# Attention chunks in groups of one and two, with masks and value swaps placed by hand, in a fused retention and low-rank mixing kernel

## The chip, the cores and the metric

The kernel runs on one core of a Trainium2 chip. The time is device microseconds of one execution; the kernel before was timed three times. In the profile PE is TensorE's matmul row and PEld its weight loads, DVE is VectorE, ACT ScalarE, POOL GpSimd, SP the engine whose queue issues most transfers. A line number such as L513 is a line of the kernel before. All times below are microseconds unless marked ns.

## The reference

Shapes: q, k, v are 8 batches x 8 heads x 576 positions x 64; the model width is 512.

```
scores = scale * q @ k.T                       # per batch and head
gamma  = 1 - 2 ** (-5 - head)
ret    = scores * where(rel >= 0, gamma ** rel, 0)
x      = ret @ v                               # heads side by side: 576 x 512 per batch

h   = (x.T @ U) @ V                            # U 576 x 32, V 32 x 576
u   = x + h.T
out = u + relu(u @ w_ch1) @ w_ch2              # 512 -> 2048 -> 512
```

Inputs and output are float32; the kernel computes in bf16 and accumulates in float32.

## The kernel before, in words

**Tiling.** Two batches form a pair, `pr` = 0 to 3, and a pair's 1152 rows are cut into 9 chunks of 128 tokens, `i` = 0 to 8. Chunk 4 (`J`) holds the last 64 rows of the first batch and the first 64 of the second. The decay factors are folded into scalings of q's side (`qscale`, on the result) and of v (`vscale`), so attention is linear: within each half chunk of 64 rows a masked product of scores and values, and across half chunks a running state, a 64 x 64 matrix per head.

**One chunk's attention.** `load` (L230) brings q, k, v by the SP queue; `prep` casts them (q on ScalarE, k on VectorE or, from the seventh chunk of pair 1 on, on GpSimd), scales v on GpSimd, and `xbar` (L263) transposes q and k by a transfer that also stands in the SP queue. Then on TensorE, all in 64 x 64 tiles, four of which share the array: `SC` (L279, scores, 16 matmuls), `ST` (L290, the state's increments, 8 or 16), `QS` (L361, q times the state, 8 or 16), `RV` (L344, masked scores times values, 16). On VectorE: `states` (L323, L325, adds an increment to the running state `s_f`, two half chunks per chunk, each from the one before), `XS` (L372, scales the result into `x`), `mask` (L303, four instructions of 64 x 256 from PSUM to `ret`), `swap_v` (L315, two copies that bring each half of v to the other 64 partitions, where RV reads them as `vs`). On ScalarE: `cast_states` (L334, the states in bf16, `s_sb`).

**A section.** `section(new, last)` joins the scores and increments of chunk n+1 with the products of chunk n: SC, ST, states, QS, RV, XS, mask, swap_v, in that order. So the masks and swaps of a chunk stand at the end of one section, and the next section's RV reads them. A full section has 64 small matmuls. PSUM: `psc` two banks (scores left, increments right), `po` two banks, `pss` one, and three banks `ps_big`, tag `big`.

**The large products.** For each batch `y1_items` makes 16 items, each the relu of 128 of the 2048 hidden columns for all the batch's chunks (4 chunks for an even batch, `par` 0, one PSUM bank; 5 for an odd one, two banks); ScalarE empties them (L518). `y2_items` makes for each chunk 4 items of 4 matmuls 128x512 into one bank, then one VectorE add (L536, `o_sb`) and a store from GpSimd's queue (L539). Both take their banks from `big`. An item carries its nominal time: 864 ns for 4 matmuls of 512 columns, 1080 ns for a Y1 item with five chunks.

**Mixing.** `MA` (L427) sums x.T U over a batch's chunks and ScalarE copies it (`a_sb`, L433); `MH` (L454) multiplies by V for groups of up to four chunks, and VectorE adds x (L460) into `u`; `MT` transposes u by a transfer on the SP queue (`uT`). An even batch has one group, an odd one two, (4,5,6) and (7,8).

**The order.** The engines' queues follow the program's order (`manual_schedule`). Startup and a first stretch make pair 0's attention and the first Y1. Then for b = 1 to 7 the large products of batch b are the `main` list, and `merge` drops the attention and mixing of batch b+1 between its items: each filler has a place, a share of the list's nominal time, and is issued before the first item at which that share is done. `places` does the same for loads and preps. Batch 1's list is 10 leftover Y1 items, then the Y2 items of batches 0 and 1 (41.9 us nominal); an even batch has 27.6, an odd one 34.6, and the Y1 half comes first. Fillers of before: sections and state casts alternate at equal steps over the first part of each list, MA, the last cast and MH follow. A tile taken from a pool takes the buffer that was released first in program order.

Of the kernel before, what the change touches and what calls it, by code (L numbers as in the profile page):

```python
# [9 lines left out]
FP32 = mybir.dt.float32  # L10
BF16 = mybir.dt.bfloat16
# [25 lines left out]
def kernel(  # L37
# [56 lines left out]
    s_f = consts.tile([P, 2, NHP * D], FP32, name="s_f")  # L94
# [21 lines left out]
    def early_consts():  # L116
# [39 lines left out]
        nc.vector.memset(sblk, 0.0)  # L156
# [115 lines left out]
    def SC(pr, i):  # L272
        c = ch[pr, i]
        qkT = c["qkT"]
        psc = ps_sc.tile([P, 2, 2 * SW], FP32, tag="psc", name="psc")
        for hp in range(NHP):
            for t in HALVES:
                for hl, r in enumerate(HALVES):
                    nc.tensor.matmul(  # L279
                        psc[t, hl, hp * D:(hp + 1) * D], qkT[r, NHP + hp, t],  # L280
                        qkT[r, hp, t], start=True, stop=True,
                    )
        c["psc"] = psc

    def ST(pr, i, steps):
        c = ch[pr, i]
        for hp in range(NHP):
            for hl, r in enumerate(HALVES):
                for t in steps:
                    nc.tensor.matmul(  # L290
                        c["psc"][r, t, SW + hp * D:SW + (hp + 1) * D],
                        c["qk"][HALVES[t], 1, hp * P + hl * HALF:hp * P + (hl + 1) * HALF],
                        c["v"][HALVES[t], 2 * hp + hl, :], start=True, stop=True,
                    )

    def mask(pr, i):
        c = ch[pr, i]
        tile_ = ret_pool.tile([P, H, P], BF16, tag="ret", name="ret")
        ret = tile_.rearrange("p h n -> p (h n)")[:, 0:2 * SW].rearrange(
            "p (t hp i) -> p t hp i", t=2, i=D)  # L300
        for hl, o in enumerate(HALVES):
            for n, t in enumerate(HALVES):
                nc.vector.tensor_tensor(  # L303
                    out=ret[o, n],
                    in0=c["psc"][t, hl, 0:SW].rearrange("p (hp i) -> p hp i", i=D),
                    in1=tri[t, None, t].to_broadcast([HALF, NHP, HALF]), op=ALU.mult,
                )
        c["ret"] = ret
# [8 lines left out]
    def states(pr, i, steps):  # L317
        c = ch[pr, i]
        f = s_f
        for t in steps:  # L320
            inc = c["psc"][:, t, SW:2 * SW]
            if (i, t) in ((0, 0), (J, 1)):
                nc.vector.tensor_copy(out=f[:, t, :], in_=inc)  # L323
            else:
                nc.vector.tensor_tensor(  # L325
                    out=f[:, t, :], in0=inc,
                    in1=f[:, 1 - t, :], op=ALU.add)
        c["s0"] = st.get("s_sb")

    def cast_states(pr, i, steps):  # L330
        w = slice(steps[0], steps[-1] + 1)
        st["s_sb"] = ch[pr, i]["s1"] = s_pool.tile(
            [P, 2, SW], BF16, tag="s_sb", name="s_sb")
        nc.scalar.activation(  # L334
            out=ch[pr, i]["s1"][:, w, :], in_=s_f[:, w, :], func=AF.Copy)

    def RV(pr, i):
        c = ch[pr, i]
        inter = q_steps(i)
        for hp in range(NHP):  # L340
            for t in range(2):
                for hl, r in enumerate(HALVES):
                    vt = c["v"][r, 2 * hp + hl, :] if t == hl else c["vs"][r, hp, :]
                    nc.tensor.matmul(  # L344
                        c["po"][HALVES[t], hl, hp * D:(hp + 1) * D],
                        c["ret"][r, t, hp, :], vt,
                        start=(hp == 0 and t not in inter), stop=True,
                        skip_group_check=True,
                    )

    def q_steps(i):
        return (1,) if i == 0 else (0,) if i == J else (0, 1)

    def QS(pr, i):
        c = ch[pr, i]
        c["po"] = ps_o.tile([P, 2, dm], FP32, tag="po", name="po")
        for hp in range(NHP):
            for t in q_steps(i):
                for hl, r in enumerate(HALVES):
                    s_sb = c["s1"][:, 0, :] if t == 1 else c["s0"][:, 1, :]  # L360
                    nc.tensor.matmul(  # L361
                        c["po"][HALVES[t], hl, hp * D:(hp + 1) * D],
                        c["qkT"][r, hp, HALVES[t]], s_sb[r, hp * D:(hp + 1) * D],
                        start=(hp == 0), stop=True, skip_group_check=True,
                    )

    def XS(pr, i):
        c = ch[pr, i]
        if ("x", pr) not in st:
            st["x", pr] = x_pool.tile([P, NI, dm], BF16, tag="x", name="xt")  # L370
# [756 lines left out]
```

## Time and profile before

| what | us |
|---|---|
| three runs, median (lowest to highest) | 319.9 (319.54 to 320.24) |
| span of the profiled execution | 318.7 |
| TensorE busy, L547 (Y2) and L513 (Y1) in it | 311.4, of which 126.3 and 132.2 |
| VectorE busy; L303 (masks), L315 (swaps) | 169.1; 45.3, 14.3 |
| ScalarE busy; L518 (Y1 drains), L334 (state casts) | 136.7; 89.1, 15.5 |
| lists of batch 1 / 2 / 3 / 4 / 5 / 6 / 7 begin near | 59 / 106 / 138 / 178 / 210 / 249 / 281 |

A row of the profile's groups reads: line, engine, operation, output <- inputs, partitions x elements and type, count, busy time, mean ns of one, then the idle time before them and what ended it. Matmuls overlap in TensorE's pipeline, so their mean ns is not what each one costs: that is read from the distance of their starts. In the chain of waits each piece has a start, a length and what ran; "issue" is time in which an engine waited for nothing that the profile shows.

### The profile page before, as it was taken

To read this page: it belongs to the slowest core of one execution; us is meant where nothing else is said; L and a number is where in the kernel's file an instruction comes from. 1 tells how busy PE (TensorE), PEld (TensorE's weight loads), DVE (VectorE), ACT (ScalarE), POOL (GpSimd) and SP (SyncE) were. 2 spreads that over 40 slices of the span, in tenths; PEclk is the share of its full clock that TensorE was granted. 3 is DMA by queue.
4 is the path that set the end of the run, shared out by engine and by line. 5 is a ranking of instruction groups with operands and counts; after the bars stand their busy time and mean duration, and the time that the engine had idled before them with its cause. 6 is when DMAs were issued, how large, how long until landed. Compare 5 with 4: busy or idle time off the path is not lost.

```text
span 318.7 us, 9166 instructions
## 1 busy us (share of the span) xinstructions
PE 311.4 (98%) x3929; PEld 167.7 (53%) x3929; DVE 169.1 (53%) x354; ACT 136.7 (43%) x293; POOL 90.3 (28%) x138
## 2 busy tenths in 40 slices
PE   8999899999999999999999999999999999999996
PEld 3564554554444444466644444466644444467544
DVE  5571466447995467545684468545674563500012
ACT  2757557772120465038720375048720463057400
POOL 5762933512232423132241423141241300110000
DMA  7999999999999979699994999598994710620022
GB/s 202 258 204 267 232 198 203 191 203 187 237 212 216 260 156 175 137 242 183 176 184 106 262 177 175 142 248 172 163 202 109 189 37 1 135 81 0 2 84 81
DMA packets 151321, 53.30 MB, mean 167 GB/s; under 512 B 131985, under 2 KB 148753, under 8 KB 151281
## 3 DMA queue, kind: packets, MB, share of 16 engines
q1 hardware_dynamic: 144512, 40.40, 70.2%
q0 software_dynamic: 6768, 12.32, 16.2%
q8 instruction: 30, 0.49, 0.7%
q14 instruction: 11, 0.08, 0.1%
HBM read 36.85 MB, written 9.44 MB: 145 GB/s over the span
## 4 chain that ended last, share of the span: by engine, by line
PE 84%; DMA 7%; ACT 3%; DVE 2%; issue 1%; SPq 1%; POOL 1%; ACTq 0%
PE ps_y L513 37%; PE ps_y L547 35%; DMA stage_t<-in_q_dram 5%; DMA qkT<-qk 2%; PE psc L279 2%; PE ph L454 1%; PE po L344 1%; PE ps_y L558 1%; PE po L361 1%; SPq L595 1%; PE psc L290 1%; PE pa L427 1%; ACT qkT L639 1%; PE psc L656 1%; PE pst L628 1%
## 5 line engine op out<-in xcount | busy, mean ns | idle before, releaser
L518 ACT ACTIVATE y<-ps_y 128x384 bf16<-128x384 f32 (+2 forms) x192 | 89.1, 489 | 105.1 <-PE ps_y L513 104.6
L513 PE MATMUL ps_y<-uT,w_sb 128*128 128x512 bf16 (+3 forms) x768 | 132.2, 326 | 0.7 <-ACT uT L922 0.4
L547 PE MATMUL ps_y<-w_sb,y 128*128 128x512 bf16 x560 | 126.3, 379 | 0.0
L513 PEld LDWEIGHTS <-w_sb 128*128 128x128 bf16 x768 | 70.2, 98 | 51.0 <-issue 2.4
L547 PEld LDWEIGHTS <-y 128*128 128x128 bf16 x560 | 52.7, 98 | 61.3
L536 DVE TENSOR_TENSOR o_sb<-ps_y,u 128x512 f32<-128x512 f32 (+2 forms) x38 | 25.2, 663 | 66.3 <-PE ps_y L547 63.9
L303 DVE TENSOR_TENSOR ret<-psc,tri 64x256 bf16<-64x256 f32 x108 | 45.3, 419 | 1.1
L539 POOL DMA_DIRECT2D out_dram<-o_sb x31 | 17.3, 558 | 98.6 <-DVE o_sb L536 95.7
L255 POOL TENSOR_TENSOR vt<-stage_t,vscale 128x512 bf16<-128x512 f32 (+1 forms) x29 | 30.2, 1041 | 52.3 <-DMA stage_t<-in_v_dram 44.6
L325 DVE TENSOR_TENSOR s_f<-psc,s_f 128x256 f32<-128x256 f32 x42 | 17.8, 423 | 26.2 <-PE psc L290 12.9
L460 DVE TENSOR_TENSOR u<-ph,xt 128x1024 bf16<-128x1024 f32 (+3 forms) x24 | 21.8, 951 | 9.3 <-PE ph L454 9.3
L246 ACT ACTIVATE qk<-stage_t 128x512 bf16<-128x512 f32 x27 | 16.9, 626 | 21.1 <-DMA stage_t<-in_q_dram 15.2
L372 DVE TENSOR_TENSOR xt<-po,qscale 128x512 bf16<-128x512 f32 x27 | 18.4, 681 | 1.8 <-PE po L344 1.8
L244 POOL CAST qk<-stage_t 128x512 bf16<-128x512 f32 x20 | 12.3, 614 | 23.6 <-DMA stage_t<-in_k_dram 21.4
L334 ACT ACTIVATE s_sb<-s_f 128x512 bf16<-128x512 f32 (+1 forms) x27 | 15.5, 575 | 3.8 <-DVE s_f L325 3.8
L315 DVE COPY vs<-vt 64x256 bf16<-64x256 bf16 x54 | 14.3, 265 | 1.2
L664 DVE TENSOR_TENSOR ret<-psc,triU 128x1024 bf16<-128x1024 f32 x8 | 9.6, 1222 | 9.2 <-PE psc L656 9.2
L189 PE MATMUL pw<-ident 128*128 128x512 bf16 x34 | 11.5, 461 | 1.4 <-POOL ident masks.py:199 1.4
L613 POOL CAST qk<-stage_t 128x512 bf16<-128x512 f32 x16 | 9.6, 613 | 9.9 <-DMA stage_t<-in_q_dram 5.3
L323 DVE COPY s_f<-psc 128x256 f32<-128x256 f32 x6 | 2.5, 424 | 16.4 <-PE psc L290 11.3
L279 PEld LDWEIGHTS <-qkT 64*64 64x64 bf16 x432 | 5.6, 107 | 9.6 <-issue 8.5
L433 ACT ACTIVATE a_sb<-pa 128x128 bf16<-128x128 f32 x8 | 2.2, 277 | 18.0 <-PE pa L427 18.0
(112 smaller groups left out, 191.4 us busy)
## 6 DMA issues: line engine op xcount, KB each, us to landing
stage_t<-in_k_dram SPq DMA_DIRECT2D x32, 256.0 KB, 4.8
stage_t<-in_q_dram SPq DMA_DIRECT2D x32, 256.0 KB, 5.3
stage_t<-in_v_dram SPq DMA_DIRECT2D x32, 256.0 KB, 5.5
out_dram<-o_sb POOLq DMA_DIRECT2D x31, 256.0 KB, 4.3
w_sb<-in_moe_w_ch_dram POOLq DMA_DIRECT2D x4, 512.0 KB, 8.0
w_sb<-in_moe_w_ch_dram POOLq DMA_DIRECT2D x8, 256.0 KB, 5.8
stage_t<-in_k_dram SPq DMA_DIRECT2D x8, 128.0 KB, 5.1
stage_t<-in_q_dram SPq DMA_DIRECT2D x8, 128.0 KB, 5.5
```

Of the source, the lines that this page charges most:

```text
L246: nc.scalar.activation(out=t[rows, 0, :], in_=c["f", 0][rows].rearrange("p h d -> p (h d)"), func=AF.Copy)
L255: (eng or nc.gpsimd).tensor_tensor(out=c["v"][rows], in0=c["f", 2][rows], in1=vscale[rows, i, :, None].to_broadcast([n, H, D]), op=ALU.mult,)
L303: nc.vector.tensor_tensor(out=ret[o, n], in0=c["psc"][t, hl, 0:SW].rearrange("p (hp i) -> p hp i", i=D), in1=tri[t, None, t].to_broadcast( ...
L325: nc.vector.tensor_tensor(out=f[:, t, :], in0=inc, in1=f[:, 1 - t, :], op=ALU.add)
L334: nc.scalar.activation(out=ch[pr, i]["s1"][:, w, :], in_=s_f[:, w, :], func=AF.Copy)
L372: nc.vector.tensor_tensor(out=xt[:, i, :].rearrange("p (hp hl d) -> p hl hp d", hl=2, d=D), in0=c["po"][:, :, 0:NHP * D].rearrange("p hl ( ...
L460: nc.vector.tensor_tensor(out=st["u", par][:, i0 - base:i0 - base + n, w].rearrange("p s (c d) -> p c s d", c=2), in0=ph[k][:, :, 0:n, :], ...
L513: nc.tensor.matmul(ps[:, 0:n, :], w1_sb[:, cc, f * P:(f + 1) * P], st["uT", par][:, c0:c0 + n, cc, :], start=(cc == 0), stop=(cc == NCC - 1),)
L518: nc.scalar.activation(out=st["y1", par][:, f, c0 * P:(c0 + n) * P], in_=ps[:, 0:n, :].rearrange("p s t -> p (s t)"), func=AF.Relu)
L536: nc.vector.tensor_tensor(out=o_sb[:, 0:n], in0=ps[:, 0:n], in1=st["u", par][:, c, w], op=ALU.add)
L539: (nc.sync if last else nc.gpsimd).dma_start(out=out_flat[r0:r0 + P, w], in_=o_sb[:, 0:n])
L547: nc.tensor.matmul(ps, st["y1", par][:, f, c * P:(c + 1) * P], w2_sb[:, f, :], start=(f == 0), stop=(f == NF - 1),)
```

## The change

Sections take a group of one or two chunks. The 27 chunks of pairs 1 to 3 are cut into 16 groups, and each step of a group, S (section), C (state cast), M (masks), W (value swaps), has a place of its own in the lists. Inside a section the products of the last group now come ahead of the scores of the new one. A group of two puts its state increments into `pss` and a `big` bank, since its scores fill `psc`; a group of one keeps both in `psc`. Mixing in these lists uses `po` for MA, and `po`, `pss` and `big` for MH, with three VectorE adds instead of two. Loads and preps have new places. `x` becomes two tiles, one per batch; `s_f` and `s_sb` hold four half chunks; three small startup tables move into tiles that are free then.

```diff
-    iotaU = consts.tile([P, 2, P], FP32, name="iotaU")
+    iotaU = s_f[:, 0, :].rearrange("p (j i) -> p j i", j=2)
...
-    sblk = consts.tile([P, 4, NHP, P], BF16, name="sblk")
-    U_f = consts.tile([P, 5, R], FP32, name="U_f")
+    s_halves = [s_pool.tile([P, 4, NHP * D], BF16, tag="s_sb", name="s_sb") for _ in range(2)]
...
+    U_f = s_f[:, 1, 0:5 * R].rearrange("p (c r) -> p c r", r=R)
...
-        nc.vector.memset(sblk, 0.0)
+        for t in s_halves:
+            nc.vector.memset(t, 0.0)
...
+    def SC(new):
         psc = ps_sc.tile([P, 2, 2 * SW], FP32, tag="psc", name="psc")
+        for a, c in enumerate(new):
+            qkT = ch[c]["qkT"]
+            for hp in range(NHP):
+                for t in HALVES:
+                    for hl, r in enumerate(HALVES):
+                        nc.tensor.matmul(
+                            psc[t, hl, a * SW + hp * D:a * SW + (hp + 1) * D],
+                            qkT[r, NHP + hp, t], qkT[r, hp, t], start=True, stop=True,
+                        )
+        return psc
+
+    def ST(new, psc):
+        if len(new) == 1:
+            inc = [psc[:, t, SW:2 * SW] for t in range(2)]
+        else:
+            inc = [ps_s.tile([P, 2 * SW], FP32, tag="pss", name="inc0"),
+                   ps_big.tile([P, 2 * SW], FP32, tag="big", name="inc1")]
...
+    def mask(new, psc):
+        m = len(new) * NHP
...
                 nc.vector.tensor_tensor(
-                    out=ret[o, n],
-                    in0=c["psc"][t, hl, 0:SW].rearrange("p (hp i) -> p hp i", i=D),
-                    in1=tri[t, None, t].to_broadcast([HALF, NHP, HALF]), op=ALU.mult,
+                    out=ret[o, n, 0:m],
+                    in0=psc[t, hl, 0:m * D].rearrange("p (b i) -> p b i", i=D),
+                    in1=tri[t, None, t].to_broadcast([HALF, m, HALF]), op=ALU.mult,
                 )
...
-        c["vs"] = s_pool.tile([P, NHP, D], BF16, tag="vs", name="vs")
+        c["vs"] = s_pool.tile([P, NHP, D], BF16, tag="vs", bufs=4, name="vs")
...
+    def states(new, inc):
+        for a, (pr, i) in enumerate(new):
+            for t in k_steps(i):
+                s, src = 2 * a + t, inc[t][:, a * SW:(a + 1) * SW]
+                if (i, t) in ((0, 0), (J, 1)):
+                    nc.vector.tensor_copy(out=s_f[:, s, :], in_=src)
+                else:
+                    nc.vector.tensor_tensor(
+                        out=s_f[:, s, :], in0=src, in1=s_f[:, st["f_end"], :], op=ALU.add)
+                st["f_end"] = s
+
+    def cast_states(new):
+        s_sb = s_pool.tile([P, 4, SW], BF16, tag="s_sb", name="s_sb")
+        n = 2 * len(new)
+        nc.scalar.activation(out=s_sb[:, 0:n, :], in_=s_f[:, 0:n, :], func=AF.Copy)
...
+    def out_products(last):
+        po = ps_o.tile([P, 2, 2 * SW], FP32, tag="po", name="po")
...
+        for a, (pr, i) in enumerate(last):
+            c = ch[pr, i]
+            for hp in range(NHP):
+                for t in q_steps(i):
...
+        for a, (pr, i) in enumerate(last):
+            c = ch[pr, i]
+            for hp in range(NHP):
+                for t in range(2):
+                    for hl, r in enumerate(HALVES):
+                        vt = c["v"][r, 2 * hp + hl, :] if t == hl else c["vs"][r, hp, :]
...
     def section(new, last):
 
+        if last:
+            po = out_products(last)
         if new:
-            SC(*new)
-            ST(*new, k_steps(new[1]))
-            states(*new, k_steps(new[1]))
-        if last:
-            QS(*last)
-            RV(*last)
-            XS(*last)
+            psc = SC(new)
+            inc = ST(new, psc)
+        for a, c in enumerate(last):
+            XS(*c, po, a)
         if new:
-            mask(*new)
-            swap_v(*new)
...
+            states(new, inc)
+            return psc
...
+        def MH(grp, beside=False):
+            lo = ps_o.tile([P, 2, NHP, P], FP32, tag="po", name="ph0")
+            if beside:
+                ph = [(lo, (0, 1)),
+                      (ps_s.tile([P, 1, NHP, P], FP32, tag="pss", name="ph1"), (2,)),
+                      (ps_big.tile([P, 1, NHP, P], FP32, tag="big", name="ph2"), (3,))]
...
-        items.append(MA)
+        items.append(lambda: MA((ps_o, "po")))
         for grp in outs:
-            items.append(lambda grp=grp: (MH(grp), MT(grp)))
+            items.append(lambda grp=grp: (MH(grp, True), MT(grp)))
...
+        stream = [(pr, i) for pr in range(1, B // 2) for i in range(NI)]
+        groups, n = [], 0
+        for size in (1, 2, 2, 1, 2, 1) + 2 * (2, 2, 1, 2, 2):
+            groups.append(stream[n:n + size])
+            n += size
...
+        def step(kind):
+            n = done[kind]
+            done[kind] += 1
+            new = groups[n] if n < len(groups) else []
+            if kind == "S":
+                scores[n] = section(new, groups[n - 1] if n else [])
+            elif kind == "C":
+                cast_states(new)
+            elif kind == "M":
+                mask(new, scores[n])
+            else:
+                for c in new:
+                    swap_v(*c)
+
         places = {
-            1: ((0.11, 0.24, 0.41, 0.53, 0.95), (0.06, 0.20, 0.32, 0.47, 0.60, 0.73)),
-            2: ((0.05, 0.18, 0.30, 0.95), (0.09, 0.29, 0.40, 0.52)),
...
+            1: ((0.11, 0.24, 0.41, 0.53, 0.70, 0.85),
+                (0.06, 0.20, 0.32, 0.47, 0.60, 0.73, 0.90)),
+            2: ((0.02, 0.14, 0.30, 0.55, 0.75), (0.05, 0.22, 0.40, 0.58, 0.85)),
+            3: ((0.02, 0.18, 0.36, 0.65, 0.90), (0.08, 0.25, 0.45, 0.62)),
+            4: ((0.15, 0.36, 0.55, 0.80), (0.05, 0.20, 0.45, 0.65, 0.88)),
+            5: ((0.02, 0.18, 0.36), (0.08, 0.25, 0.45, 0.62)),
+        }
+        fills = {
+            1: ("S.22 C.24 M.24 W.25 S.42 C.44 M.45 W.49 S.58 C.60 M.61 W.66 "
+                "S.70 C.73 M.74 W.80 S.96 C.98 M1 W1", (0.74, 0.78)),
+            2: ("S.25 C.28 M.27 W.30 S.52 C.55 M.75 W.80 S.90 C.94 M1 W1", (0.58, 0.64, 0.70)),
+            3: ("S.25 C.28 M.27 W.30 S.52 C.54 M.71 W.75 S.90 C.94 M1 W1", (0.58, 0.65)),
+            4: ("S.52 C.55 M.75 W.80 S.90 C.94 M1 W1", (0.58, 0.64, 0.70)),
+            5: ("S.25 C.28 M.27 W.30 S.52 C.54 M.71 W.75 S.90 C.94 M1 W1", (0.58, 0.65)),
+            6: ("S.20", (0.35, 0.45, 0.50)),
         }
```

In `fills` the letters are the steps with their places (shares of the list), and the numbers behind them are the places of MA and of each MH. "1" puts a step behind the list's last item. S.70 below means the section at 0.70 of its list.

More of the change, by code (lines that the diff above doesn't have):

```diff
@@ L296, in mask, with x_of, k_steps, q_steps @@
-    def mask(pr, i):
-        c = ch[pr, i]
+    def x_of(pr, i, n=None):
+        half = int(i >= J)
+        if ("x", pr, half) not in st:
+            st["x", pr, half] = x_pool.tile(
+                [P, NI - J if half else J, dm], BF16, tag=f"x{half}", name="xt")
+        t, l = st["x", pr, half], i - J * half
+        return t[:, l, :] if n is None else t[:, l:l + n, :]
+    def k_steps(i):
+        return (1,) if i == J else (0,) if i == NI - 1 else (0, 1)
+    def q_steps(i):
+        return (1,) if i == 0 else (0,) if i == J else (0, 1)
@@ L315, in swap_v @@
             nc.vector.tensor_copy(out=c["vs"][o], in_=v[HALVES[1 - hl], hl])
[L317 to L370, printed above, removed]
-        xt = st["x", pr]
+    def states(new, inc):
+        for a, (pr, i) in enumerate(new):
+            for t in k_steps(i):
+                s, src = 2 * a + t, inc[t][:, a * SW:(a + 1) * SW]
[5 more added lines that the diff above has]
+                st["f_end"] = s
@@ L1096 @@
             merge(main, fill, aux)
+        assert done["S"] == len(groups) + 1
         assert gl == len(order) and gp == len(order)
```

138 lines of the change are left out of this document (66 added, 72 removed), and 4 rows, old and new, of the table places.

## The prediction

> **What bounds the kernel now.** I read four views in this order: the busy table with the chain that ended last, that chain in order of time, TensorE's timeline through one attention section, and VectorE's timeline. The page first:
>
> ```profile
> PE 311.4 (98%) x3929; PEld 167.7 (53%) x3929; DVE 169.1 (53%) x354; ACT 136.7 (43%) x293; POOL 90.3 (28%) x138
> PE 84%; DMA 7%; ACT 3%; DVE 2%; issue 1%; SPq 1%; POOL 1%; ACTq 0%
> L761 DVE TENSOR_TENSOR ret<-psc,tri 64x512 bf16<-64x512 f32 x2 | 1.4, 689 | 5.2 <-PE psc L752 5.2
> ```
>
> TensorE is the bound; every other engine has half its time free on average. (The third line, from the groups by shape, is a price used below.) The chain in order of time (start, length, what) gives TensorE's own rates, and the places where it waits:
>
> ```profile
> 84.11 7.26 DMA qkT<-qk
> ...
> 131.11 7.01 PE ps_y L547 x32
> ...
> 142.80 0.46 ACT y L518
> 143.26 0.26 issue
> 143.52 0.62 ACT s_sb L334
> 144.14 0.52 ACT qk L246
> 144.66 0.39 ACT y L518
> ...
> 168.97 8.74 PE ps_y L547 x40
> ```
>
> 8 more Y2 matmuls cost 8.74 - 7.01 = 1.73 us, so 0.216 each, and 0.10 is left over per stretch (7.01 - 32 x 0.216). At 142.8 the chain leaves TensorE: two Scalar Engine jobs (cast of states, cast of q) stand between Y1 drains, and the Y1 stretch is 0.34 us longer than its matmuls. TensorE's timeline through a section:
>
> ```profile
> 145.61 0.32 PE L279 MATMUL psc<-qkT 64*64 64x64 bf16 x16
> 145.76 0.30 PE L290 MATMUL psc<-vt,qk 64*64 64x64 bf16 x16
> 145.89 0.30 PE L361 MATMUL po<-s_sb,qkT 64*64 64x64 bf16 x16
> ...
> 146.26 0.34 PE L513 MATMUL ps_y<-uT,w_sb 128*128 128x384 bf16 x1
> ```
>
> 16 small matmuls start in 0.13 us (145.76 to 145.89), so 64 take 0.52. From the first (145.61) to the next Y1 matmul (146.26) is 0.65, and with the 0.10 that each stretch carries a section costs 0.75, of which 0.23 is a price per section and not per matmul. VectorE's timeline behind a section, and one bad case with GpSimd beside it:
>
> ```profile
> 73.32 0.89 DVE L325 TENSOR_TENSOR s_f<-psc,s_f 128x256 f32<-128x256 f32 x2 [1.85 <-PE po L361]
> 74.12 0.68 DVE L372 TENSOR_TENSOR xt<-po,qscale 128x512 bf16<-128x512 f32 x1
> 74.72 1.72 DVE L303 TENSOR_TENSOR ret<-psc,tri 64x256 bf16<-64x256 f32 x4
> 76.47 0.46 DVE L315 COPY vs<-vt 64x256 bf16<-64x256 bf16 x2
> 76.96 0.69 DVE L536 TENSOR_TENSOR o_sb<-ps_y,u 128x512 f32<-128x512 f32 x1
> 77.56 0.42 DVE L244 CAST qk<-stage_t 128x512 bf16<-128x512 f32 x1
> ...
> 160.13 1.25 DVE L315 COPY vs<-vt 64x256 bf16<-64x256 bf16 x2
> ```
>
> ```profile
> 160.25 1.04 POOL L255 TENSOR_TENSOR vt<-stage_t,vscale 128x512 bf16<-128x512 f32 x1 [1.61 <-DMA stage_t<-in_v_dram]
> ```
>
> Start to start: states 0.45 where one adds to the other, x scaling (XS) 0.60, four masks 1.75, two swaps 0.49, output add 0.60, k cast 0.34. A pair doubles states, XS and swaps; its four masks become 64x512, the shape of L761, 0.69 each: 2.8.
>
> **The change, part by part.**
>
> Sections. The old plan runs 28 (27 chunks plus a last one without a new chunk); the new one has 16 groups, so 17. Matmuls per chunk stay the same in number and shape. Saved: 11 x 0.23 = 2.53 us. Bursts grow to at most 128 small matmuls, which no row shows. If they keep the rate, 2.53 stands; if the second half of the ten pair bursts started at half rate, it would cost 10 x 0.25 = 2.5 and nothing would be left. I take the full rate, since the four groups of 16 above show none slower than the first.
>
> Old waits that go. The 0.34 at 142.8 and its twin at 214.4: casts of states now come once in a Y1 stretch, alone, not beside a q cast; a lone cast costs 0.03 there (stretches from 146.26 and 151.35). Three times the second mixing group has waited for VectorE to empty the two tiles of the first: 8 mixing matmuls took 0.22 at 51.56 but 0.36 at 130.67, so 0.14; with three smaller tiles, freed in turn, two of the three vanish (batches 3 and 5). The section at 91.42 waited 0.18 for the qkT transfer issued at 84.11, which is covered by the wait below. Together 0.68 + 0.28 + 0.18 = 1.14.
>
> New wait 1, the fourth section of batch 1's stretch (S.70). Take t = 0 at the start of the section before it (S.58, at a chunk's end). On VectorE: output add 0.20 to 0.80, two XS to 2.0, three states to 3.25, a k cast still on VectorE for this chunk to 3.6, four wide masks to 6.4, the next output add to 7.0, then the swaps: first chunk done 7.5, second 8.0. TensorE needs 30 groups of 4 (0.96) + 0.23 = 1.19, six Y2 items of 0.864, and 0.19 for the state products: it wants the first swapped values at 6.56 and would finish at 6.82; it finishes at 8.14. Loss 1.3. The transfer of 84.11 lands at 91.4, when by these sums TensorE is at that section (91.3) and waiting anyway. W.66 stands behind the masks and the output add on one queue; that is the price of queueing it late. Bounds: 0 if VectorE is 1.3 faster, 2.1 if one swap is held up as at 160.13 (1.02 instead of 0.22).
>
> New wait 2, S.90 of batches 2 and 4 (masks at .75, swaps at .80): the same count puts the second chunk's swaps 0.3 after TensorE wants them. 2 x 0.3 = 0.6, bounds 0 to 2.2 (a held swap of 0.8 each).
>
> New wait 3, the last mixing. The two groups stand one Y1 item apart (.45 and .50, 15 and 16 items done), 0.96 us. VectorE's three adds for the first (128x768, 0.95; 128x384, an estimate of 0.55 between 0.42 for 256 and 0.68 for 512 columns) free the tiles after 1.1, 1.57 and 2.04. The second group waits 0.6, and the next Y2 chunk, whose PSUM buffer is the one freed last, 0.15. Against the 0.14 before: +0.6.
>
> New wait 4: S.96 stands one item before batch 2's Y1. Its second state tile sits in a Y1/Y2 bank until 2.93 after its start, when TensorE wants it at 2.72: 0.2. The double state cast (128x1024; L334 gives 0.62 for half of it, so about 1.1) is hidden, because Y1 with 4 chunks tolerates a drain 0.8 late; in batches 3 and 5 two more Y2 items lie between. Uncovered it would cost 0.5 each time.
>
> Costed at nothing, with their cover: products before scores (state casts, masks and swaps are all one section old); mixing first stage in the other bank (XS is done at 2.2 where it starts at 2.8); load and prep times moved (each load still stands 6 us or more before its prep, and median landing is 4.8 to 5.5 us; at the closest, batch 2's first load, a landing of 6.0, as of the q load issued at 112.57, would hold Y1's drains by some 0.5, within what they tolerate). The SP queue keeps its order up to the seventh transpose, past which one load (three DMAs, 2 us) moves, with 5 us to spare. GpSimd's queue is not reordered against its loads. The startup edits touch only where small tables lie; two memsets for one.
>
> **Sum.** -2.53 - 1.14 + 1.3 + 0.6 + 0.6 + 0.2 = -1.0 us. On the profiled execution's 318.7 us span that is 317.7. The runs' median, 319.9, lies 1.2 above this span, so 318.9 for the runs. A difference under 0.2%, 0.64 us, can't be told from none.
>
> **The Trainium skill** (SBUF — State Buffer, section "Who interferes with whom") says that VectorE copies in their fast modes and GpSimd share one port pair as an exclusive lock, and the later one blocks for a whole instruction. The trace agrees at 160.13: the swap beside GpSimd's 1.04 us instruction took 1.02, not 0.22. By that rule, this rival follows.
>
> **Rivals.** *Swaps held up by GpSimd (slower).* Swaps now end just ahead of the section that reads them, at S.58, S.70 and twice S.90. Each one that meets a GpSimd instruction adds 0.8 there: three of them make +2.4, so 321.3. It decides from two on (-1.0 + 1.6 = +0.6). For: 5 of the 54 swaps on VectorE's timeline were held up so, by 0.08 to 0.80. Against: near S.70 and S.90 GpSimd's scaling is done or waits behind an output store. Chance 0.17.
>
> *Banks in strict turn (slower).* If the three Y1/Y2 buffers went round in order rather than by first freed, the third Y2 chunk of batches 2 and 4 would need the buffer of the chunk just ended, whose output add stands behind the mixing adds: 1.25 each, 321.4. For: mixing and state tiles now share these three. Against: nothing else in the old Y stretches took buffers out of turn, so no row decides. Chance 0.07.
>
> *VectorE keeps up (faster).* If masks overlap as XS and output adds do (0.60 apart), or the sections come later than I count, waits 1 and 2 go: 318.9 - 1.9 = 317.0. For: VectorE is 53% busy. Against: the masks stand 0.44 apart for 0.42 each, so they don't overlap. Chance 0.14.
>
> *Long bursts lose what the merging saves (it doesn't do what it says).* With 0.1 per pair burst, or batch 1 paced by its transfers whatever the order, 1.0 is lost: 319.9. For: the transfers' share in that stretch is above 1 (16 engines' mean) and the chain passes through qkT there. Chance 0.12.
>
> **Chances.** Forecast 0.50, own range 318.2 to 319.7. Faster by 0.64: three quarters of the forecast, all of the third rival and little else, 0.53. Same: the rest of the forecast and most of the fourth, 0.23. Slower: both slow rivals, 0.24. The range that leaves out 2 in 10: 316.9 to 321.4.
>
> **What would show it.** Right: 17 bursts; pair bursts of 0.9 to 1.15 us; a gap of about 1.3 inside the products of S.70 that ends with L315's successor; mixing's last second group 0.8 instead of 0.36; no wait at the Y1 starts of batches 3 and 5. Wrong: swaps over 0.5 us ahead of a section, a wait of TensorE on an output add at a chunk's start, or burst rates above 0.032 us per four. I would be wrong most likely at VectorE's queue, whose order I counted by hand.

## The result, and the profile after

The kernel after takes 322.88 us (median of 20 runs, 320.81 to 327.06), the kernel before 320.35 (20 runs). The ratio is 1.0074 with an interval of 1.0046 to 1.0101: 0.7% slower, where 318.9 was forecast. Medians are over all runs of a kernel, and ratios leave disturbed executions of either kernel out, so the two can differ a little.

The profiled execution took 325.31 us with a span of 323.3, one of the slower of its 20. The page of the kernel after:

```profile
PE 309.7 (96%) x3903; PEld 169.8 (53%) x3929; DVE 167.6 (52%) x320; ACT 137.8 (43%) x282; POOL 90.6 (28%) x138
...
PEclk9999999999998999999999999999999999999999
...
PE 80%; DMA 7%; SPq 5%; DVE 5%; issue 3%; ACT 0%; POOL 0%; DVEq 0%
```

TensorE is still busy for some 310 us, so the change did not add work: the span grew by waiting. A line has appeared that the page before did not have, TensorE's granted clock, with a dip in slice 13. (26 matmul records are missing from this trace; the weight loads, 3929 as before, are complete, and stretches below are measured by them.) TensorE's waits from 60 us to the end, in total, times and longest:

```profile
PE po L388 <- DVE vs L340: 2.5, 2, 1.8
PE ps_y L559 <- issue: 2.4, 14, 0.3
PE psc L297 <- DMA qkT<-qk: 0.6, 1, 0.6
PE ps_y L525 <- DVE s_f L349: 0.2, 1, 0.2
PE ph L465 <- DVE u L471: 0.2, 1, 0.2
```

The second line is the missing records. The first is the section at .70 of batch 1 (S.70): its products of masked scores and values, RV (L388), wait for the swaps (L340). The chain in order of time shows that place:

```profile
91.80 0.69 DVE o_sb L548
...
92.52 0.22 DVE vs L340
...
92.75 0.22 DVE vs L340
...
93.01 0.55 DVE vs L340
93.56 0.01 issue
93.57 1.57 DVE vs L340
95.14 0.04 issue
95.18 0.31 PE po L388 x15
```

TensorE reached the swapped values at 92.2 and had them all at 95.2. Four equal swaps take 0.22, 0.22, 0.55 and 1.57. GpSimd's timeline says why:

```profile
92.78 0.58 POOL L551 DMA_DIRECT2D out_dram<-o_sb  x1 [4.70 <-DVE o_sb L548]
93.37 0.66 POOL L247 CAST qk<-stage_t 128x512 bf16<-128x512 f32 x1
94.01 1.03 POOL L258 TENSOR_TENSOR vt<-stage_t,vscale 128x512 bf16<-128x512 f32 x1
```

The output add at 91.80 stands just ahead of the swaps on VectorE. When it ends, it releases GpSimd's store, and behind the store wait the k cast and v scaling of chunk (1,7), the first chunk of pair 1 whose k GpSimd casts: they run beside the last two swaps and hold them up. The two waits are 0.84 and 2.02, together 2.9. The two held swaps took 0.33 and 1.35 longer than the 0.22 of the others, so 1.7 of the 2.9 is GpSimd's hold; the remaining 1.2 is VectorE's queue, which came to the swaps late. Then comes a second loss. Stretches of the trace (start and end, length, TensorE busy and its instructions, granted clock, transfer share, GB/s):

```profile
92.00:95.00 3.00, 0.70 (x41) 1.00 1.25 141
95.00:96.00 1.00, 0.63 (x47) 0.77 0.94 245
96.00:97.00 1.00, 0.86 (x3) 0.50 1.26 280
97.00:98.00 1.00, 1.00 (x4) 0.50 0.41 97
98.00:99.00 1.00, 1.00 (x4) 0.52 0.98 219
99.00:100.00 1.00, 1.00 (x24) 1.00 0.08 18
```

After 3 us in which TensorE was busy for 0.70, its clock is halved. What the four stretches from 95 to 99 miss of the full clock adds up to 1.71, so half the clock lasts 3.4 us. The eight Y2 matmuls that fall there start 0.427 apart instead of 0.216: 3.4 us instead of 1.7, another 1.7. One such dip takes the mean clock of a run to 0.995. Ten of the 20 runs have a mean clock of 0.995 or less, with a median of 324.1; the other ten have 322.1, still 1.8 above the kernel before.

The other new wait is in batch 4, at S.90. The chain there:

```profile
206.04 0.27 PE ph L465 x8
...
206.91 0.42 DVE u L471
207.33 0.26 SPq L483
...
208.06 4.92 DMA qkT<-qk
```

The transposes of q and k (prep at .65) stand on the SP queue behind the transposes of u (L483), which wait for the mixing's adds. TensorE waits 0.76 (0.6 in the list above, which counts from the end of the last matmul).

### The profile page after: what moved, and what is told of

The parts are those of the page before. It is cut to its first block, busy times and chain, and to the rows that moved or that the text cites. A ratio compares the mean times of both kernels' runs of the same rounds, so it can differ in the third digit from the quotient of the medians.

```text
span 323.3 us, 9091 instructions
## 1 busy us (share of the span) xinstructions
PE 309.7 (96%) x3903; PEld 169.8 (53%) x3929; DVE 167.6 (52%) x320; ACT 137.8 (43%) x282; POOL 90.6 (28%) x138
## 4 chain that ended last, share of the span: by engine, by line
PE 80%; DMA 7%; SPq 5%; DVE 5%; issue 3%; ACT 0%; POOL 0%; DVEq 0%
PE ps_y L525 36%; PE ps_y L559 34%; DMA w_sb<-in_moe_w_ch_dram 3%; SPq L605 3%; DMA stage_t<-in_v_dram 2%; DMA qkT<-qk 2%; SPq L233 1%; PE po L377 1%; PE po L388 1%; PE ph L465 1%; PE psc L297 1%; PE ps_y L570 1%; PE pa L431 1%; PE inc L314 1%; DVE ret L327 1%
## 5 line engine op out<-in xcount | busy, mean ns | idle before, releaser
L525 PE MATMUL ps_y<-uT,w_sb 128*128 128x512 bf16 (+3 forms) x768 | 130.4, 326 | 1.6 <-DMA w_sb<-in_moe_w_ch_dram 0.9
L559 PE MATMUL ps_y<-w_sb,y 128*128 128x512 bf16 x534 | 123.8, 382 | 3.0 <-issue 2.4
L551 POOL DMA_DIRECT2D out_dram<-o_sb x31 | 17.4, 562 | 130.9 <-DVE o_sb L548 126.6
L356 ACT ACTIVATE s_sb<-s_f 128x1024 bf16<-128x1024 f32 (+1 forms) x16 | 14.8, 922 | 89.8 <-DVE s_f L349 83.2
L327 DVE TENSOR_TENSOR ret<-psc,tri 64x512 bf16<-64x512 f32 (+1 forms) x64 | 38.6, 602 | 1.2
L471 DVE TENSOR_TENSOR u<-ph,xt 128x512 bf16<-128x512 f32 (+4 forms) x33 | 22.3, 732 | 13.6 <-PE ph L465 13.6
L340 DVE COPY vs<-vt 64x256 bf16<-64x256 bf16 x54 | 16.9, 313 | 1.0
L349 DVE TENSOR_TENSOR s_f<-inc,s_f 128x256 f32<-128x256 f32 x38 | 16.1, 423 | 1.7
L388 PE MATMUL po<-vs,ret 64*64 64x64 bf16 x216 | 7.3, 195 | 2.5 <-DVE vs L340 2.5
L627 POOL TENSOR_TENSOR qk<-stage_t,vscaleU 128x512 bf16<-128x512 f32 x7 | 7.3, 1054 | 4.2 <-DMA stage_t<-in_v_dram 4.2
L377 PEld LDWEIGHTS <-qkT 64*64 64x64 bf16 x384 | 4.7, 108 | 6.3 <-issue 5.9
```

Source lines behind the costliest of these rows:

```text
L327: nc.vector.tensor_tensor(out=ret[o, n, 0:m], in0=psc[t, hl, 0:m * D].rearrange("p (b i) -> p b i", i=D), in1=tri[t, None, t].to_broadcast ...
L340: nc.vector.tensor_copy(out=c["vs"][o], in_=v[HALVES[1 - hl], hl])
L349: nc.vector.tensor_tensor(out=s_f[:, s, :], in0=src, in1=s_f[:, st["f_end"], :], op=ALU.add)
L471: nc.vector.tensor_tensor(out=st["u", par][:, i0 - base:i0 - base + n, w].rearrange("p s (c d) -> p c s d", c=len(ccs)), in0=t[:, :, 0:n, ...
L525: nc.tensor.matmul(ps[:, 0:n, :], w1_sb[:, cc, f * P:(f + 1) * P], st["uT", par][:, c0:c0 + n, cc, :], start=(cc == 0), stop=(cc == NCC - 1),)
L551: (nc.sync if last else nc.gpsimd).dma_start(out=out_flat[r0:r0 + P, w], in_=o_sb[:, 0:n])
```

## The experiments

A list's length below is the distance from its first Y1 weight load to the next list's. Runs made together share their runs of the kernel before; its median was 319.9 to 321.2 from session to session, so ratios are compared rather than medians. The time to the first section varies by up to 1.8 us from trace to trace (e13 and e14), so single spans are not compared either.

**Whose wait is it at S.70?** Three kernels after with one edit each.

```diff
- S.58 C.60 M.61 W.66        # e1_swaps_first: swaps ahead of masks
+ S.58 W.59 C.60 M.61
+ if last[0] == (1, 3): warm(8)   # e2_filled_wait: between QS and RV, results not used
- 1: (..., 0.60, 0.73, 0.90)      # e3_prep_later: prep of (1,7)
+ 1: (..., 0.60, 0.78, 0.90)
```

> Only the place of the third group's value swaps moves: W.66 to W.59, ahead of its masks on VectorE. Theory A (the swaps end too late for S.70, and the wait lets TensorE's clock fall): no wait inside S.70's products (2.9 us in the profile of the changed kernel, 0.84 us of work in 3.8), granted clock 1.000, no Y2 matmul at 0.427 us; runs 2.5 to 4 us below the changed kernel's 322.9, so near 319.5 and a little below the kernel before. Theory B (the transfer of the next chunk's qkT paces this stretch whatever the order): S.70 waits for qkT instead and at most 1 us is won, near 322.

> The late swaps stay; 8 throwaway matmuls of 512 columns (8 x 0.216 = 1.7 us) stand in S.70 between the state products and the products that need the swaps, results unused. Theory A (the clock falls because TensorE idles): the section stays as long as it was, 3.5 to 4 us, but the granted clock is 1.000 and the Y2 matmuls behind it start 0.216 apart, not 0.427; runs with a clock of 0.995 vanish and the median is about 1 us lower, 322. Theory B (the fall has another cause): 0.995 and 0.427 stay, median 322.9 or more.

> Only the place of the seventh chunk's prep of pair 1 moves, 0.73 to 0.78, so its GpSimd cast and scaling come behind another output store. Theory A (GpSimd's two instructions hold the swaps up by the shared port, 2.6 us for four copies): the four swaps take about 1 us again, the wait in S.70 is 1.1 to 1.5 us as the prediction had it, the clock stays at 1.000, median 320.5 to 321.5. Theory B (the queue order alone makes them late): swaps and wait as before, 2.6 and 2.9, median 322.9.

e1: 321.25 us, ratio 1.0026 (1.0007 to 1.0045). The section's wait falls from 2.9 to 1.3, now on the masks, and none of its 12 runs shows the lower clock. (A further 0.5 stands in this trace at S.58, whose swaps take 1.73 beside GpSimd's scaling.) So the late swaps cost about 0.5% of the 0.7, and something is left.

e2: 323.23, ratio 1.008 (1.005 to 1.011), no better. Its trace shows full clock from 92 to 102 us with the Y2 matmuls 0.216 apart, so filling the wait does keep the clock there; but the same trace lost the clock in the startup (0.76 from 17 to 24 us), and two of its six runs have a mean of 0.995 or less. What the fill is worth in time stays open.

e3: 324.1, ratio 1.0116 (1.0078 to 1.0154), slower still: the later prep made the next section wait 2.45 for the transposed q and k of (1,7), and three of its six runs have the lower clock. Its use is on VectorE's timeline, where nothing of GpSimd but the store's issue (0.58) meets the swaps:

```profile
87.14 1.13 DVE L247 CAST qk<-stage_t 128x512 bf16<-128x512 f32 x1
...
91.04 0.69 DVE L548 TENSOR_TENSOR o_sb<-ps_y,u 128x512 f32<-128x512 f32 x1
91.76 0.94 DVE L340 COPY vs<-vt 64x256 bf16<-64x256 bf16 x4
```

The four swaps take 0.94 instead of 2.61: without GpSimd's cast and scaling beside them they aren't held. TensorE's wait is still 1.9 (1.50 and 0.36), since GpSimd held VectorE up at another place. The k cast at 87.14, ahead of the masks, took 1.13 instead of 0.42 beside the scaling of another chunk's v:

```profile
86.94 1.04 POOL L258 TENSOR_TENSOR vt<-stage_t,vscale 128x512 bf16<-128x512 f32 x1 [1.26 <-DMA stage_t<-in_v_dram]
```

Without these 0.7 it would be 1.2, by subtraction. So VectorE's own queue is worth 1.2 in e3, 1.2 in the kernel after and 1.3 in e1, and the other 1.7 of the 2.9 is GpSimd holding two swaps.

**All waits that the trace shows, moved.**

```diff
- 1: "S.42 C.44 M.45 W.49 S.58 C.60 M.61 W.66 ..."   4: prep 0.65   6: mixing (0.35, 0.45, 0.50)
+ 1: "S.42 W.43 C.44 M.45 S.58 W.59 C.60 M.61 ..."   4: prep 0.58   6: mixing (0.35, 0.42, 0.50)
```

> Four places moved: W.66 to W.59 and W.49 to W.43 (swaps ahead of masks), batch 4's prep of the fourth chunk 0.65 to 0.58 (ahead of the mixing's transposes on SP), the last mixing's second stage 0.45 to 0.42 (two Y1 items apart). If the waits of the changed kernel are these and add up: 2.9 + 1.0 (clock, mean) + 0.2 + 0.8 + 0.5, so 317.5 to 318.5 and 0.6 to 0.9% below the kernel before. If a new wait stands behind each removed one: not under 319.5.

320.23 us, ratio 1.0001 (0.9974 to 1.0027). List 4 is 0.7 shorter than after's (31.84 against 32.56), list 6 is 0.6 shorter (29.64 against 30.24). Those two waits are as read. But with most of the new waits gone (S.70 still waits 1.2 for its masks, and a section of list 2 now 0.5 for its transposed q and k) the kernel is only level with the kernel before, so part of the gain that should have remained is missing.

**What does a merged section save?** Eight pair sections of e4 cut in two again.

```diff
- 2: "... S.52 C.55 ... S.90 C.94 M1 W1"
+ 2: "... P.52 T.54 C.55 ... P.90 T.92 C.94 M1 W1"   # P products, T scores and increments
```

> The kernel of e4_all_moved with eight pair sections of batches 2 to 5 cut in two again: the products (and x scaling) at the old place, the scores and increments one large-product item later. Nothing else moves. Theory A, the step of the prediction (each section carries a price of 0.23 us whatever its length): 8 x 0.23 = 1.84 us longer than e4, lists 2 to 5 longer by 0.46 each; 322.1. Theory B, from the traces (a pair burst of 128 takes 1.30, two single ones 2 x 0.64, because the small matmuls slow down after the first 50 or so; only the 0.10 of the stretch is saved): 8 x 0.09 = 0.7 us longer, 0.17 per list, 320.9, and both halves of each cut section start their matmuls in fours 0.032 apart.

321.64 us, ratio 1.0000 (0.9974 to 1.0027). Lists 3 and 5, where no cut section waits, are 0.32 and 0.34 longer for two cuts each, of which the state bank at the next Y1 takes about 0.1 and 0.07. That is 0.12 per section, between the theories but near B. TensorE's timeline of e4 shows a pair section, and that of e8 the same section cut (start, length, what; the starts matter):

```profile
175.39 0.45 PE L377 MATMUL po<-s_sb,qkT 64*64 64x64 bf16 x32
...
175.97 0.50 PE L297 MATMUL psc<-qkT 64*64 64x64 bf16 x32
176.29 0.45 PE L314 MATMUL inc<-vt,qk 64*64 64x64 bf16 x24
176.68 0.60 PE L559 MATMUL ps_y<-w_sb,y 128*128 128x512 bf16 x2
```

```profile
176.00 0.45 PE L377 MATMUL po<-s_sb,qkT 64*64 64x64 bf16 x32
...
176.69 1.04 PE L559 MATMUL ps_y<-w_sb,y 128*128 128x512 bf16 x4
177.66 0.45 PE L297 MATMUL psc<-qkT 64*64 64x64 bf16 x32
177.93 0.42 PE L314 MATMUL inc<-vt,qk 64*64 64x64 bf16 x24
178.29 0.39 PE L559 MATMUL ps_y<-w_sb,y 128*128 128x512 bf16 x1
```

32 score matmuls take 0.32 in the pair (175.97 to 176.29) and 0.27 behind the cut (177.66 to 177.93). The whole pair is 1.29, its two halves 0.69 and 0.63. So inside the burst a merge saves almost nothing: from 60 us on, and without the waits over 0.2, the bursts of the kernel after add up to 17.4 us in 17 sections and those of the kernel before to 17.2 in 28. Saved is the 0.10 that a stretch of large products carries. A merge is therefore worth 0.08 by the bursts and 0.12 by e8, some 0.1.

**Do the old waits go without any merging?** The kernel before, with mixing's three tiles, and the first prep of lists 3 and 5 a little later.

```diff
- 3, 5: preps (0.11, 0.18, ...)
+ 3, 5: preps (0.14, 0.18, ...)     # e9_before_two_fixes
+ 3, 5: preps (0.13, 0.18, ...)     # e11_before_fixes_kept_order
- items.append(lambda grp=grp: (MH(grp), MT(grp)))
+ items.append(lambda grp=grp: (MH(grp, True), MT(grp)))
```

> The kernel before, sections single and in their old places, with two small parts of the change alone: mixing's products in three tiles (po, pss, big) with three adds, and in lists 3 and 5 the first prep at 0.14 instead of 0.11, so that its q cast no longer stands beside the state cast. If the prediction's second term is right (waits that go without any merging): lists 2 and 4 shorter by 0.14 each, lists 3 and 5 by 0.31 each, 0.9 in all: 319.5 against 320.4. Rival (the waits only move to the next Y1 drain or to the next user of the Y bank): no change, 320.4.

> As e9_before_two_fixes, but the moved prep at 0.13: still one large-product item later than in the kernel before, yet ahead of the load at 0.14 in the SP queue, as there. In e9 the load had come ahead of the transposes. If that order alone made e9's lists 3 and 5 longer, they are now 0.31 shorter each than in the kernel before (39.3 instead of 39.6), lists 2 and 4 0.1 each, 0.8 in all, ratio 0.9975. If the later q cast itself is the trouble (it meets the next prep's cast and holds the Y1 drains), lists 3 and 5 stay longer than 39.6.

e9: 323.17 us, ratio 1.0069 (1.0031 to 1.0106). The two waits went (second mixing group 0.22 instead of 0.36; the Y1 stretch that had 0.44 extra has 0.13), but list 3 grew by 0.5 us and list 5 by 3.5. SP's queue in list 5, and then TensorE's wait there:

```profile
216.06 0.38 SPq L230 DMA_DIRECT2D stage_t<-in_k_dram  x1
...
218.72 6.06 SPq L263 DMA_TRANSPOSE qkT<-qk  x3
```

```profile
PE psc L279 <- DMA qkT<-qk: 2.1, 1, 2.1
```

At .14 the load comes ahead of the transposes, which in the kernel before are issued from 216.34, before that load. Directly behind the wait of 2.1 the granted clock falls to a half from 224.7 to 228.1, which costs another 1.7. With the order kept (e11) list 3 is 39.28 instead of 39.60, the 0.31 expected, and lists 2 and 4 are 0.30 and 0.14 shorter, but list 5 is 39.89 instead of 39.59: there a Y1 drain on ScalarE holds TensorE for 0.3. So about half of the 0.8 is in the trace. The median is 320.45 against 320.51, ratio 0.9999 (0.9979 to 1.0020): gains of this size in one trace are not found in the runs.

**Take S.70's remaining wait away.** e4 with that section later, singles instead of pairs, or loads elsewhere. The kernels with singles also place these sections, and e14 to e16 some preps and loads of lists 1 and 2, anew.

```diff
- 1: "... S.70 C.73 M.74 W.80 S.96 C.98 M1 W1", (0.74, 0.78)
+ 1: "... S.74 C.77 M.78 W.79 S.92 C.95 M1 W1", (0.78, 0.82)   # e10_later_fourth
+ 1: "... S.74 C.77 M.78 W.79 S.96 C.98 M1 W1", (0.78, 0.82)   # e12_fourth_only
- for size in (1, 2, 2, 1, 2, 1) + 2 * (2, 2, 1, 2, 2):
+ for size in 9 * (1,) + 2 * (2, 2, 1, 2, 2):                  # e13_singles_first, e14
+ for size in 10 * (1,) + (2, 1, 1, 2, 2) + (2, 2, 1, 2, 2):   # e16_pairs_from_third
- 1: loads (..., 0.53, 0.70, 0.85)
+ 1: loads (..., 0.53, 0.95)                                   # e14_singles_old_loads, e16
+ 1: loads (..., 0.53, 0.84, 0.95)                             # e15_loads_behind_u: e12 with this
```

> The kernel of e4_all_moved with batch 1's fourth section at .74 instead of .70 (its casts, masks, swaps and the mixing behind it .04 later) and the fifth at .92 instead of .96. If VectorE's masks and adds are what the fourth section waits for (1.2 us in e4) and the late state bank holds up batch 2's first Y1 items (0.4): both go, 1.6 less, 318.6. Rival (the transfers of the chunks pace batch 1): the fourth section waits no more but the fifth waits for its transposed q and k, at least 1 us, and the time stays at 320.2.

> The kernel of e4_all_moved with the fourth section at .74 as in e10, the fifth left at .96. Theory VectorE: the fourth section waited 1.2 us for masks in e4, that goes, and the fifth, two items later than in e10, has its transposed q and k in time: 1.2 less than e4, ratio 0.9965 to before. Rival (the transfers pace batch 1, as e10's fifth section with its 1.8 us wait suggests): the fifth section waits 0.5 to 1 us again, and half of the gain is left or none.

> The kernel of e4_all_moved with all nine chunks of pair 1 (lists 1 and 2) in groups of one, their masks and swaps right behind the section as in the kernel before; pairs 2 and 3 stay grouped in ones and twos. Theory: grouping saves only about 0.1 us per section, and all that e4 still loses is in lists 1 and 2 (1.2 at the fourth section, 0.4 for transposed q and k, 0.4 at batch 2's Y1). Then, against the kernel before, without the startup: -0.3 mixing, -0.6 casts beside a q cast, -0.2 the old wait for transfers, -0.7 for seven sections fewer, +0.3 for the state bank at two Y1 starts: -1.5, ratio 0.995. Rival (the transfers pace lists 1 and 2, whatever TensorE saves): the sections of list 2 wait for qkT, -0.5 at most, ratio 0.998 to 1.

> The kernel of e13_singles_first with the loads and preps of list 1 back at the places of the kernel before (the load of chunk (1,8) at .95, behind the transposes of u, instead of .70, ahead of them), those of list 2 a little closer together so that its sections still find their chunks. In e13 that load took the queue and the transfer engines from 95 to 103 us, u's transposes landed at 109.1 (103.8 in the kernel before), and batch 2's first Y1 waited 1.3 us for them. Theory (the moved loads are what list 1 loses): the Y1 wait of 1.3 and the 0.7 for transposed q and k at the sixth section go, list 2 starts as early after the first section as in the kernel before, -1.5 in all, ratio 0.995. Rival (the transfers of lists 1 and 2 together are the limit): the same wait comes back in list 2, at the sections of chunks (1,8) or (2,0), ratio 0.998 or more.

> The kernel of e12_fourth_only (ones and twos) with list 1's last two loads at .84 and .95 instead of .70 and .85, so behind the transposes of u, and two preps a little later for it. Theory as for e14: u's transposes land by 105 instead of 108.2, batch 2's first Y1 waits no 1.2 us for them, the 0.8 for transposed q and k in list 2 shrinks: 1.5 less than e12, ratio 0.996. Rival: the later load makes list 2's first section (chunk (1,8)) or second wait by as much, ratio 1.000 as e12.

> The kernel of e14_singles_old_loads with list 2's section at .52 for chunk (2,0) alone, as in the kernel before, and pairs from list 2's last section on. In e14 that section took (2,0) and (2,1) together and waited 2.2 us for the transposed q and k of (2,1), issued at .33. Theory (pairing asks for the second chunk a whole section earlier, where the transfers of lists 1 and 2 have no room; grouping itself is harmless and worth 0.1 a section): no wait for transfers is left, -1.5 against the kernel before without the startup, ratio 0.995. Rival (the transfers of lists 1 and 2 are the limit however they are asked for): a wait for qkT of 0.5 us or more again, in list 2 or early in list 3, ratio 0.998 or more.

The waits are those of the profile's list, where nothing else is said; e10's measures 1.8 by the weight loads.

| kernel | ratio (interval) | S.70 or its like | where a wait came back |
|---|---|---|---|
| e10 | 0.9975 (0.9936 to 1.0014) | none | 1.6 for qkT at the fifth section |
| e12 | 1.0003 (0.9978 to 1.0027) | none | 1.2 for uT at batch 2's Y1, 0.8 for qkT in list 2 |
| e13 | 0.9994 (0.9968 to 1.0021) | 0.7 by the weight loads, 0.5 of it for qkT | 1.3 for uT at batch 2's Y1 |
| e14 | 1.0043 (1.0011 to 1.0074) | none | 2.2 for qkT at list 2's first pair |
| e15 | 1.0086 (1.0055 to 1.0117) | none | 2.4 for Y1's drains on ScalarE, 0.9 for qkT |
| e16 | 1.0028 (0.9996 to 1.0060) | 0.4 by the weight loads | 1.3 for uT at batch 3's Y1, 0.9 for drains, 0.8 unnamed in a section of list 3 |

VectorE's wait at S.70 can be taken away by moving the section by .04, and each time another wait takes its place. Over all runs, none of these kernels shows the theory's gain of 1.2 to 1.6 us. e10's five runs with full clock have a median of 319.1, the lowest here and 1.7 below the 25 full-clock runs of the kernel before beside them (320.8), but seven of its 12 lost the clock. The seven have 324.2. Five runs picked by their outcome don't show a gain, though.

**Amount or order of the transfers?** e12 and the kernel before, both without the stores of batches 0 to 2.

```diff
+            if 2 * pr + par > 2:
                 (nc.sync if last else nc.gpsimd).dma_start(
```

> The kernel of e12_fourth_only without the output stores of batches 0 to 2 (these outputs are left out; the adds stay), which takes 13 x 0.26 MB of transfers and GpSimd's 13 store instructions out of lists 1 and 2. Theory (the transfers of lists 1 and 2 have no room, so what TensorE saves there comes back as a wait): e12's waits of lists 1 and 2 for u's transposes (1.2) and for transposed q and k (0.8) vanish, and the same change is now worth what TensorE saves: 1 to 1.5 less than e18_before_no_stores. Rival (the order of the SP queue makes those waits, not the amount): 1 us or more of them stays, and e17 is no shorter than e18.

> The kernel before without the output stores of batches 0 to 2 (left out as in e17_fourth_no_stores). Both theories: its one wait for a transfer in lists 1 and 2 (0.18 at the sixth section) goes and nothing else changes there, since TensorE bounds it: 320.4, the same as the kernel before within 0.3.

TensorE's waits for transfers in e12 from 60 us on:

```profile
PE ps_y L525 <- DMA uT<-u: 1.2, 1, 1.2
PE psc L297 <- DMA qkT<-qk: 0.8, 1, 0.8
```

and all its waits in e17 (the first line is 26 missing matmul records again):

```profile
PE ps_y L560 <- issue: 1.9, 12, 0.2
PE ps_y L525 <- DVE s_f L349: 0.2, 1, 0.2
```

Both waits for transposes are gone. e17 takes 319.25 us, ratio 0.9948 (0.9927 to 0.9970) to the kernel before, e18 320.35, ratio 0.9992 (0.9967 to 1.0018). Without these stores the changed plan is worth 1.1 us of the median, and the kernel before gains nothing that can be measured. u's transposes for batch 2 are issued at the same place of list 1 in both (42.9 after its start) and land 4.3 after their issue in e17 and 6.6 in e12. So the order of the SP queue alone doesn't make them late; the stores do. In e12 three loads and the transposes of q and k ahead of u's are issued later than in e17, and those transposes are still in flight when u's are issued. The edit takes the stores' transfers and GpSimd's 13 store instructions out together, so which of the two it is stays open; u's transposes do not pass through GpSimd. In the kernel before they land at 103.8, 1.9 ahead of batch 2's Y1.

No version here with all its work beats the kernel before by more than its interval.

## Why the prediction was wrong

The forecast was 1.0 us less. Measured is 1.8 more in the runs that kept the clock, and 2.5 more in the median. Three steps failed: the price saved per section, the swaps taken to be free of GpSimd, and a clock that can fall, which the sum did not have.

- **"If they keep the rate, 2.53 stands"** failed first: 11 merges save some 0.1 each, 1.1 in all. Of the price of 0.23 only the 0.10 of the stretch is saved. The four groups of 16 that were looked at are a whole burst of the kernel before, and none of its bursts is longer; in most pair bursts pauses come from about the 46th matmul on and cost what the missing break saves. Pair bursts without a long wait take 1.2 to 1.4, not 0.9 to 1.15. The rival "long bursts lose what the merging saves" named it, with a chance of 0.12 and 1.0 us; it measured 1.4.
- **New wait 1**: the place, the queue and the count were right. VectorE's queue makes 1.2 to 1.3 (after, e1, e4), as forecast. What stood on top, 1.7, is what that paragraph had as a bound alone, swaps held by GpSimd: 2.1 for one held swap there, 2.9 for two here.
- **The slow rival was argued away with a wrong sentence**: "near S.70 and S.90 GpSimd's scaling is done or waits behind an output store". It does wait behind one, and the add that releases that store stands directly ahead of the swaps, so the scaling is set free exactly then. That is for the rival, not against it. Two swaps were held, by 0.33 and 1.35, where the rival had 0.8 each. One place was enough, since a long wait has a price of its own:
- **The halved clock was not among the costs** (1.7 in the profiled run; half of the runs have a mean clock that fits one such dip).
- **New wait 2** (2 x 0.3): none in batch 2, 0.76 in batch 4 for another reason. "The SP queue keeps its order up to the seventh transpose" is true of batch 1, but batch 4's prep was moved behind the transposes of u. Moving it back took 0.7 out of list 4 (e4).
- **New wait 3** held: the second mixing group takes 0.68 instead of 0.22 and the next Y item 0.15 more, 0.6 in all, and e4 took it out of list 6. **New wait 4** was 0.4 instead of 0.2 at batch 2, and 0.1 more came at batch 3's Y1, where none was expected.
- **Old waits that go** held in lists 2 to 4 (e9, e11); in list 5 of e11 a drain wait took the gain's place. In the kernel after this term was not measured by itself.
- **"Costed at nothing: load and prep times moved"** held in the profiled run, but not by the cover it was given: once S.70's wait is gone, u's transposes are 1.2 late (e12).

Sum with the measured sizes, the old waits as forecast: -1.1 - 1.1 + 2.9 + 1.7 + 0.8 + 0.5 + 0.5 = +4.2, against +4.6 between the two spans, of which 0.3 is startup. In runs that keep the clock it is 1.7 less.

## What to carry to other kernels

Price a merged burst by a burst of that length, not by the shorter ones at hand. When work is queued late on one engine, list what the instruction just ahead of it releases on the others: here one add started both a swap and the GpSimd work that blocks it. And before TensorE is made faster in a stretch, ask how late its transfers already are there: where transposes land just in time, a saving comes back as a wait for them.

## What the hardware did that was not expected

- **Waits of 2 us can halve the clock.** Three traces show the granted clock at a half, each time for 3.4 us: the kernel after, directly behind S.70's waits; e9, directly behind its wait of 2.1; e2, in the startup. Each dip costs 1.7, which makes a mean clock of 0.995. Runs with such a mean or less: 36 of 74 for the kernels whose trace has a wait of 1.6 to 2.3 us (after, e3, e9, e10, e14, e15); 7 of 108 for those with waits up to 1.3 (e1, e4, e8, e11, e12, e13, e16, e17, e18); 12 of 154 for the kernel before in the sessions of the experiments. The mean doesn't say where in a run the clock fell, and e3, e10, e14 and e15 kept the full clock in the very trace that shows the wait: so a wait of 2 us makes the dip likely, not certain. The Trainium skill (TensorE: Matmul & The Clock Gate, "HAM oscillation — how this bites in real kernels") warns of idle gaps over some 3.4 us. The half rate agrees (0.427 between starts), the limit does not: shorter waits were enough here in about half of the executions.
- **Small matmuls pause within a burst.** The first 32 of 64 x 64 start in fours 0.032 apart. After about 45 they come singly, 0.008 apart, which is the same rate; but in most pair bursts nearly every sixteenth start then takes 0.034 instead of 0.008, so 16 take 0.159 instead of 0.127. The bursts of the kernel before, 64 at most, have no such pause, and one of 88 in the kernel after (at 224.92) has none either. Behind a long wait or a few large matmuls they start in fours again (e3 after its 2.45, e8). What makes the pauses no run here shows.
- **GpSimd's store instruction doesn't hold a swap up**, its cast and its scaling do: beside the store alone four swaps take 0.94 (e3), beside cast and scaling the last two take 2.1 (after). A k cast on VectorE beside the scaling took 1.13 instead of 0.42 (e3).
- **Transposes by transfer** differ much in time from issue to landing. u's for batch 2 take 4.3 in e17, 4.9 in the kernel before and 6.6 in e12; those of q and k take 3.2 to 7.1 in the kernel before between 90 and 130 us.
